# Gate vector's product before the first turn of x, half-turn copies and another order of the first K pieces, in a fused linear-attention and MLP kernel

## The chip, the cores and the metric

The kernel runs on one core of one Trainium2 chip. The metric is the device time of one execution in microseconds, as the median of several runs. Beside the timed runs there is one profiled execution, taken by the hardware profiler; its span is the time from the first to the last instruction, and its own device time is a little longer than the span. The engines are named as in the profile: PE (matmuls) and PEld (its weight loads), DVE (vector engine), ACT (scalar engine, activations), POOL, and SP, which here only issues DMAs.

## The reference

Two branches work on the same x (2048 rows of 640 features, bf16) and are mixed by a gate per row. Branch A is linear attention with 32 heads, branch B a spatial-shift mixer with an MLP. Shortened:

```python
x = A_x
g = sigmoid((x * gate_w).sum(-1, keepdims=True))

# A: linear attention
q, k, v = split(x @ wqkv)                       # 32 heads of 20
pq, pk = phi(q), phi(k)                         # phi(t) = where(t > 0, t + 1, exp(t)) + 1e-6
kv, z = pk^T v, sum(pk)                         # per head
a = ((pq @ kv) / (pq . z + 1e-6)) @ wo

# B: layernorm, w1, gelu, shifts along the sequence, w2, residual, layernorm, w3, gelu, w4
x1 = x + shifted(gelu(layernorm(x) @ w1)) @ w2
b = x1 + gelu(layernorm(x1) @ w3) @ w4

out = g * a + (1 - g) * b
```

The part that matters here is the very first: `k = x @ wk` and the gate's row sum `x . gate_w`, which the kernel computes as one extra column of the same product.

## The kernel before

The 2048 rows are 16 chunks of 128 (c = 0 to 15), the 640 features 5 groups of 128 (dc = 0 to 4). The order of the work is written out by hand: each engine does its instructions in program order, and waits are put in by the framework where tiles depend on each other.

**The start.** x chunk 0 and chunk 1 are loaded row by row into `x_sb` (line 123, SP's queue); the later chunks come already transposed by DMA into `xT` (line 126). The five row groups of the K weights `wk_sb` are loaded alternately from SP's and ACT's queue (line 129): rows 1 on SP, rows 0 and 2 on ACT, rows 3 on SP, rows 4 on ACT. The gate vector is loaded as `g5` (5 x 128) and put into the zeroed tile `g5z` by DVE (lines 205, 206).

**Fillers.** `warmup` (line 203) issues matmuls of constants into a PSUM pair that nobody reads. Five of 512 columns and one of 384 run while the first loads are under way; later one of 512 and one of 256 columns stand between the real matmuls.

**Turns.** K products need x with the features on the partitions. For chunks 0 and 1, PE turns x itself: `turn` (lines 210 to 221) multiplies each 128 x 128 block by the identity (line 214), features 0 and 1 into the first bank of a PSUM pair, features 2, 3 and 4 into the second. Two copies (line 219) bring them to `xT`: for chunk 0 both on DVE, for chunk 1 the first on DVE and the second on ACT. In chunk 0's turn, the product of `g5z` and the identity (line 217) puts the gate vector into the first bank behind features 0 and 1, and DVE copies it into column D of `wk_sb` (line 221).

**K pieces.** A piece (c, dc) is two matmuls (line 190) that add the product of feature group dc of chunk c to a PSUM pair; the second half has the gate column as its 321st. Each chunk needs five pieces. For chunks 0 and 1 the pieces are interleaved by a list, and chunk 1's turn stands in it ahead of the third piece. Then `k_evac` (line 193) copies the gate's column with ACT and applies phi: ACT's exp (line 182) and two DVE instructions (lines 183, 184). For chunks 2 to 15 all five pieces of a chunk run in a row. PSUM has four pairs in rotation; a pair is taken again when its readers are done.

After the 16 chunks follow the Q products (line 245), the products of phi(k) with x (line 345), and branch B, all as long rows of matmuls.

Of the kernel before, what the change touches and what calls it, by code (L numbers as in the profile page):

```python
# [16 lines left out]
def kernel(  # L17
# [13 lines left out]
    nc = tc.nc  # L31
    P = 128
    S, D = A_x.shape[1], A_x.shape[2]
# [6 lines left out]
    DC = D // P  # L40
# [29 lines left out]
    def pair():  # L70
        return ps.tile([P, 2, 512], F32, name="pp")
# [17 lines left out]
    ident = const.tile([P, P], BF16)  # L89
    g5 = const.tile([DC, P], BF16)  # L90
    g5z = const.tile([P, P], BF16)
# [20 lines left out]
    wk_sb = st1.tile([P, DC, D + 16], BF16)  # L112
    gT = wk_sb
    xT = st1.tile([P, DC, S], BF16)
# [71 lines left out]
    def k_mm(pt, c, dcs, first=0, last=DC - 1):  # L186
        for dc in dcs:
            for hf in range(2):
                n = HD + hf
                nc.tensor.matmul(pt[:, hf, 0:n], lhsT=xT[:, dc, c * P:(c + 1) * P],  # L190
                                 rhs=wk_sb[:, dc, hf * HD:hf * HD + n], start=(dc == first), stop=(dc == last))
# [5 lines left out]
    k0_order = (1, 0, 2, 3, 4)  # L197
    warm = pair()
    one = nc.const_aps.tensor(1.0, (P, TS), BF16)

    def warmup(n, w=TS, pt=warm):
        for i in range(n):
            nc.tensor.matmul(pt[:, 1, 0:w], lhsT=one[:, 0:P], rhs=one[:, 0:w], start=True, stop=True)
# [1 line left out]
    nc.vector.memset(g5z[:], 0.0)  # L205
    nc.vector.tensor_copy(g5z[0:DC, :], g5[:])
    warmup(5)
    warmup(1, 3 * P)

    def turn(pt, c, split, copies):  # L210
        parts = ((0, split), (split, DC))
        for h, (a, b) in enumerate(parts):
            for dc in range(a, b):
                nc.tensor.matmul(pt[:, h, (dc - a) * P:(dc - a + 1) * P], lhsT=x_sb[:, c, dc * P:(dc + 1) * P],
                                 rhs=ident[:], start=True, stop=True)
        if c == 0:
            nc.tensor.matmul(pt[:, 0, 2 * P:2 * P + DC], lhsT=g5z[:], rhs=ident[:, 0:DC], start=True, stop=True)
        for h, (a, b) in enumerate(parts):
            copies[h](xT[:, a:b, c * P:(c + 1) * P], pt[:, h, 0:(b - a) * P].rearrange("p (c s) -> p c s", c=b - a))  # L219
            if c == 0 and h == 0:  # L220
                copies[h](wk_sb[:, :, D], pt[:, 0, 2 * P:2 * P + DC])

    tp = pair()
    turn(tp, 0, 2, (nc.vector.tensor_copy, nc.vector.tensor_copy))
    warmup(1, TS)
    kps = [pair(), pair()]
    for n, (c, dc) in enumerate(((0, 1), (0, 0), (0, 2), (0, 3), (1, 1), (1, 0), (0, 4), (1, 2), (1, 3), (1, 4))):
        if n == 2:
            turn(warm, 1, 2, (nc.vector.tensor_copy, nc.scalar.copy))
        if n == 1:  # L230
            warmup(1, 2 * P, kps[1])
        k_mm(kps[c], c, (dc,), first=k0_order[0], last=k0_order[-1])
    for c in range(2):
        k_evac(kps[c], c)
    for c in range(2, NCH):
        pt = pair()
# [481 lines left out]
```

## Time and profile before

| what | value |
|---|---|
| median of 3 runs | 262.87 us |
| the runs | 261.99, 262.87, 265.05 us |
| profiled execution, its own time | 261.71 us |
| profiled execution, span | 260.0 us |
| granted PE clock over the span | 1.000 |
| PE idle before a DMA-fed turn of chunk 0 / chunk 1 (weight load, line 214) | 0.51 / 0.22 us |
| DMA engines, mean busy share in the first 10 us, moved | 2.11 MB at 211 GB/s |
| a K matmul of 320 columns (line 190), mean of 160 | 300 ns |

The duration of a matmul in the profile includes its way through the array; in a row of them the next starts before the one ahead has ended, so the distance between starts is shorter than the duration. In the timeline, equal instructions that follow each other are merged into one line with their count; the first two numbers are the start and the time to the end of the last of them, in microseconds from the start of the span. The bracket at a line's end gives the idle time of that engine before it and whose end released it.

### The profile page before, as it was taken

Reading aid. Unit: us, or ns where it says so; the run is one execution under the profiler, and the core shown is the slowest. Engines: PE = TensorE matmul, PEld = TensorE weight load, DVE = VectorE, ACT = ScalarE, POOL = GpSimd, SP = SyncE. Lnnn points to the kernel's source line nnn. Section 1 sums busy time; section 2 is a strip of 40 time slices with the busy share of each in tenths; the row PEclk is TensorE's granted clock in tenths of the full one; section 3 lists DMA queues with packets and bytes.
Section 4 is the critical chain, followed back from the end, with each engine's and each line's share of the span. In section 5 each row is a group of like instructions: output and inputs, shape, how many; then the busy total and the mean of one; then the engine's idle time right before and its main releaser. Section 6 shows DMA issues by size and latency. Waiting matters only on the chain.

```text
span 260.0 us, 4128 instructions
## 1 busy us (share of the span) xinstructions
PE 254.9 (98%) x1590; PEld 151.0 (58%) x1613; DVE 148.1 (57%) x274; ACT 107.7 (41%) x166; POOL 32.2 (12%) x87
## 2 busy tenths in 40 slices
PE   8999999999999999999999999999999999999995
PEld 4777555788754644565464566455565546465543
DVE  2688678899998888399300398600287610125132
ACT  2655554385787547431343323342322344342100
POOL 3000040023411140023000131000122000000000
PEclk9999999999999999999999999999999999999999
DMA  7999995026661877964122124214123412211011
GB/s 217 191 204 377 363 331 203 0 43 123 122 115 31 231 77 160 283 187 84 20 43 40 20 53 96 76 23 62 20 50 74 101 20 43 48 38 57 21 50 50
DMA packets 57557, 28.27 MB, mean 109 GB/s; under 512 B 45506, under 2 KB 56770, under 8 KB 57538
## 3 DMA queue, kind: packets, MB, share of 16 engines
q1 hardware_dynamic: 57096, 27.52, 43.2%
q10 hardware_dynamic: 442, 0.49, 0.5%
q8 instruction: 12, 0.20, 0.3%
q14 instruction: 7, 0.06, 0.1%
HBM read 13.03 MB, written 3.60 MB: 64 GB/s over the span
## 4 chain that ended last, share of the span: by engine, by line
PE 96%; DMA 1%; issue 1%; SPq 0%; DVE 0%
PE pp L541 21%; PE pp L580 16%; PE pp L491 8%; PE pp L345 8%; PE pp L522 8%; PE pp L245 8%; PE pp L400 8%; PE pp L190 8%; PE pp L616 5%; DMA wk_sb<-in_A_wqkv_dram 1%; PE pp L551 1%; PE pp L572 1%; PE pp L433 1%; PE pp L419 1%; SPq L123 0%
## 5 line engine op out<-in xcount | busy, mean ns | idle before, releaser
L541 PE MATMUL pp<-lnxT,w_sb 128*128 128x512 bf16 x249 | 59.8, 379 | 0.6
L543 ACT ACTIVATE h<-pp 128x1024 bf16<-128x1024 f32 (+1 forms) x28 | 26.9, 962 | 56.0 <-PE pp L541 56.0
L580 PE MATMUL pp<-h,w_sb 128*128 128x512 bf16 (+1 forms) x228 | 42.4, 343 | 0.3
L541 PEld LDWEIGHTS <-w_sb 128*128 128x128 bf16 x260 | 25.2, 98 | 26.9
L494 DVE TENSOR_TENSOR x<-pp,x_sb 128x640 f32<-128x640 f32 x16 | 13.0, 815 | 40.0 <-PE pp L491 40.0
L580 PEld LDWEIGHTS <-w_sb 128*128 128x128 bf16 x234 | 22.7, 98 | 19.5 <-issue 1.0
L182 ACT ACTIVATE e<-pp 128x640 bf16<-128x640 f32 (+1 forms) x26 | 21.5, 827 | 9.5 <-PE pp L245 9.5
L308 POOL TENSOR_SCALAR rstd<-mv 128x1 f32<-128x1 f32 (+2 forms) x22 | 9.2, 416 | 128.8 <-DVE mv L314 127.9
L522 PE MATMUL pp<-m_sb,pqT 128*128 128x320 bf16 x160 | 24.3, 299 | 0.0
L528 DVE SCALAR_TENSOR_TENSOR x<-pp,gate,x 128x640 f32<-128x640 f32 x16 | 14.1, 882 | 17.4 <-PE pp L522 11.9
L491 PE MATMUL pp<-w_sb,hsT 128*128 128x320 bf16 x160 | 23.9, 299 | 0.0
L190 PE MATMUL pp<-wk_sb,xT 128*128 128x320 bf16 (+1 forms) x160 | 22.4, 300 | 0.2
L345 PE MATMUL pp<-x_sb,pk 128*128 128x320 bf16 (+1 forms) x160 | 22.0, 300 | 0.0
L245 PE MATMUL pp<-xT,hsT 128*128 128x512 bf16 x98 | 21.6, 379 | 0.1
L345 PEld LDWEIGHTS <-pk 128*128 128x128 bf16 x160 | 18.8, 117 | 3.2
L491 PEld LDWEIGHTS <-hsT 128*128 128x128 bf16 x160 | 15.6, 98 | 8.2 <-issue 0.2
L522 PEld LDWEIGHTS <-pqT 128*128 128x128 bf16 x160 | 15.7, 98 | 7.7
L593 DVE SCALAR_TENSOR_TENSOR oc<-pqT,omg,x 128x640 bf16<-128x640 bf16 x12 | 10.5, 878 | 16.8 <-DMA pqT<-hx 16.8
L190 PEld LDWEIGHTS <-xT 128*128 128x128 bf16 x160 | 15.5, 98 | 6.8 <-DVE xT L219 0.6
L400 PE MATMUL pp<-lnxT,w_sb 128*128 128x512 bf16 x77 | 17.9, 379 | 0.2
L245 PEld LDWEIGHTS <-hsT 128*128 128x128 bf16 x100 | 11.8, 118 | 9.7
L309 POOL TENSOR_TENSOR rstd<-rstd,mhalf 128x1 f32<-128x1 f32 (+2 forms) x22 | 16.8, 765 | 1.8
(89 smaller groups left out, 250.7 us busy)
## 6 DMA issues: line engine op xcount, KB each, us to landing
x_sb<-in_A_x_dram SPq DMA_DIRECT2D x1, 2240.0 KB
out_dram<-oc SPq DMA_DIRECT2D x14, 160.0 KB, 1.8
w_sb<-in_B_w_dram SPq DMA_DIRECT2D x1, 2160.0 KB
w_sb<-in_B_w_dram SPq DMA_DIRECT2D x1, 2080.0 KB
wo_sb<-in_A_wo_dram SPq DMA_DIRECT2D x6, 160.0 KB
hsT<-in_A_wqkv_dram SPq DMA_DIRECT2D x1, 800.0 KB
m_sb<-in_A_wqkv_dram SPq DMA_DIRECT2D x1, 800.0 KB, 12.7
w_sb<-in_B_w_dram SPq DMA_DIRECT2D x1, 800.0 KB
```

The lines of the kernel that those rows point to most:

```text
L182: nc.scalar.activation(ev, src, ACT.Exp)
L190: nc.tensor.matmul(pt[:, hf, 0:n], lhsT=xT[:, dc, c * P:(c + 1) * P], rhs=wk_sb[:, dc, hf * HD:hf * HD + n], start=(dc == first), stop=(dc ...
L245: nc.tensor.matmul(pt[:, t % 2, :], lhsT=wq_sb[:, dc, :].rearrange("p (m j) -> p j m", j=DC)[:, j], rhs=xT[:, dc, t * TS:(t + 1) * TS], st ...
L309: nc.gpsimd.tensor_tensor(out_ap, out_ap, mhalf[:, 0:out_ap.shape[1]], op=ALU.pow)
L345: nc.tensor.matmul(pt[:, hf, 0:HD + hf], lhsT=w, rhs=x_sb[:, c, hf * HD:(hf + 1) * HD + hf], start=(c == 0), stop=(c == NCH - 1))
L400: nc.tensor.matmul(pt[:, i, :], lhsT=w, rhs=lnxT[t][:, dc, :], start=(dc == 0), stop=(dc == DC - 1))
L491: nc.tensor.matmul(pt[:, hf, 0:HD], lhsT=hsT[:, fc, 2 + c * P:2 + (c + 1) * P], rhs=w2_sb[:, fc, hf * HD:(hf + 1) * HD], start=(fc == 0), ...
L522: nc.tensor.matmul(pt[:, hf, 0:HD], lhsT=pqT[:, j, c * P:(c + 1) * P], rhs=m_sb[:, j, hf * HD:(hf + 1) * HD], start=(j == 0), stop=(j == D ...
L528: nc.vector.scalar_tensor_tensor(x1, pt[:, :, 0:HD], gate[:, c:c + 1], x1, op0=ALU.mult, op1=ALU.add)
L541: nc.tensor.matmul(pt[:, k, :], lhsT=w3_sb[:, dc, fc * P:(fc + 1) * P], rhs=lnT[:, dc, :], start=(dc == 0), stop=(dc == DC - 1))
L543: nc.scalar.activation(h2[:, 2 * i * TS:(2 * i + n) * TS], pt[:].rearrange("p h e -> p (h e)")[:, 0:n * TS], ACT.Gelu_apprx_tanh)
L580: nc.tensor.matmul(dst, lhsT=w4_sb[:, fc, d * P:(d + 1) * P], rhs=st[t]["h2"][:, fc * TS + a:fc * TS + b], start=False, stop=(fc == FF - 1))
```

## The change

Three things are changed in the stretch between the first fillers and the K pieces of chunk 1.

The gate vector's product no longer belongs to chunk 0's turn. It stands ahead of it, writes into the pair `warm` that the fillers use, and is followed by a filler of 128 columns in place of the one of 384. DVE's copy into column D of `wk_sb` is issued there too.

`turn` issues the copy of each half right behind that half's products instead of behind all five, and the first half takes feature 1 before feature 0 (`range(split - 1, -1, -1)`).

In the list of K pieces, (1,1) and (1,0) stand ahead of (0,3), and (1,2) ahead of (0,4). The 256-column filler stands behind the second piece instead of ahead of it.

```diff
     warmup(5)
-    warmup(1, 3 * P)
+    nc.tensor.matmul(warm[:, 0, 0:DC], lhsT=g5z[:], rhs=ident[:, 0:DC], start=True, stop=True)
+    warmup(1, P)
+    nc.vector.tensor_copy(wk_sb[:, :, D], warm[:, 0, 0:DC])
 
     def turn(pt, c, split, copies):
-        parts = ((0, split), (split, DC))
-        for h, (a, b) in enumerate(parts):
-            for dc in range(a, b):
+        for h, dcs in enumerate((range(split - 1, -1, -1), range(split, DC))):
+            a = min(dcs)
+            for dc in dcs:
                 nc.tensor.matmul(pt[:, h, (dc - a) * P:(dc - a + 1) * P], lhsT=x_sb[:, c, dc * P:(dc + 1) * P],
                                  rhs=ident[:], start=True, stop=True)
-        if c == 0:
-            nc.tensor.matmul(pt[:, 0, 2 * P:2 * P + DC], lhsT=g5z[:], rhs=ident[:, 0:DC], start=True, stop=True)
-        for h, (a, b) in enumerate(parts):
-            copies[h](xT[:, a:b, c * P:(c + 1) * P], pt[:, h, 0:(b - a) * P].rearrange("p (c s) -> p c s", c=b - a))
-            if c == 0 and h == 0:
-                copies[h](wk_sb[:, :, D], pt[:, 0, 2 * P:2 * P + DC])
+            n = len(dcs)
+            copies[h](xT[:, a:a + n, c * P:(c + 1) * P], pt[:, h, 0:n * P].rearrange("p (c s) -> p c s", c=n))
...
-    for n, (c, dc) in enumerate(((0, 1), (0, 0), (0, 2), (0, 3), (1, 1), (1, 0), (0, 4), (1, 2), (1, 3), (1, 4))):
+    for n, (c, dc) in enumerate(((0, 1), (0, 0), (0, 2), (1, 1), (1, 0), (0, 3), (1, 2), (0, 4), (1, 3), (1, 4))):
         if n == 2:
             turn(warm, 1, 2, (nc.vector.tensor_copy, nc.scalar.copy))
+        k_mm(kps[c], c, (dc,), first=k0_order[0], last=k0_order[-1])
         if n == 1:
             warmup(1, 2 * P, kps[1])
-        k_mm(kps[c], c, (dc,), first=k0_order[0], last=k0_order[-1])
```

## The prediction

> **What bounds the kernel now.** I read the page's busy shares and the chain of waits first, then the timeline of the first 8 us, because every instruction that the change touches runs there. The page:
>
> ```profile
> span 260.0 us, 4128 instructions
> PE 254.9 (98%) x1590; PEld 151.0 (58%) x1613; DVE 148.1 (57%) x274; ACT 107.7 (41%) x166; POOL 32.2 (12%) x87
> PE 96%; DMA 1%; issue 1%; SPq 0%; DVE 0%
> ```
>
> TensorE (PE) sets the end; only work that moves the start of its unbroken stream can matter. The chain in order of time says where that stream starts:
>
> ```profile
> 1.71 0.42 SPq L123
> 2.18 3.81 DMA wk_sb<-in_A_wqkv_dram
> 6.03 21.14 PE pp L190 x154
> ```
>
> From 6.03 on PE never stops for long, and the piece that starts there had waited for the load of wk_sb rows 3 (issued at 2.18, landed at 5.99). So what counts is one date: when PE has done the ten K pieces of chunks 0 and 1 and turns to chunk 2. Two matmuls make a piece; 21.14 us / 154 = 0.137 us each, so a piece is 0.275 us. Before, six matmuls lie ahead of 6.03 and 14 behind it: the date is 6.03 + 14 x 0.137 = 7.95 us. A shift of this date shifts everything behind it. The timeline ahead of it:
>
> ```profile
> 2.73 1.28 ACT L219 ACT_TABLE_LOAD   x1 [2.73 <-issue]
> ...
> 3.15 0.56 PEld L214 LDWEIGHTS <-x_sb 128*128 128x128 bf16 x5 [0.51 <-DMA x_sb<-in_A_x_dram]
> 3.24 0.74 PE L214 MATMUL pp<-ident,x_sb 128*128 128x128 bf16 x5
> ...
> 3.77 0.21 PE L217 MATMUL pp<-ident,g5z 128*128 128x5 bf16 x1
> ...
> 3.84 0.59 PE L203 MATMUL pp<-const-bfloat16-1.0 128*128 128x512 bf16 x1
> 4.04 0.42 DVE L219 CAST xT<-pp 128x256 bf16<-128x256 f32 x1 [1.63 <-PE pp L217]
> 4.39 0.17 DVE L221 CAST wk_sb<-pp 128x5 bf16<-128x5 f32 x1
> 4.46 0.55 DVE L219 CAST xT<-pp 128x384 bf16<-128x384 f32 x1
> 4.52 0.11 PEld L190 LDWEIGHTS <-xT 128*128 128x128 bf16 x2 [0.60 <-DVE xT L219]
> 4.53 0.45 PE L190 MATMUL pp<-wk_sb,xT 128*128 128x320 bf16 x2
> ...
> 5.24 0.28 PEld L214 LDWEIGHTS <-x_sb 128*128 128x128 bf16 x5 [0.22 <-DMA x_sb<-in_A_x_dram]
> 5.25 0.45 PE L214 MATMUL pp<-ident,x_sb 128*128 128x128 bf16 x5
> ...
> 5.74 0.42 DVE L219 CAST xT<-pp 128x256 bf16<-128x256 f32 x1 [0.73 <-PE pp L214]
> ...
> 6.19 0.48 ACT L219 CAST xT<-pp 128x384 bf16<-128x384 f32 x1 [2.18 <-DVE xT L219]
> ```
>
> Columns: start, duration, engine, line, operation, and in brackets the idle time before it and who ended it. Three things to see. The first copy of a turn starts only after the last product of the turn (4.04 after L217; 5.74 after the fifth product). Chunk 1's turn starts at 5.25 because its x has just landed. ACT's table load of 1.28 us waits for nothing and lies in dead time, 2.2 us before ACT's copy.
>
> **The change, part by part.** No DMA, no SP or POOL instruction moves and no work is added in sum; 256 columns of filler go, matmuls change place, and waits change.
>
> *Gate product first.* It goes behind the five fillers, where g5z has been ready since 2.42. The x rows land at 3.15 in any case and a 128-column filler fills until then, so the turn starts at 3.16 to 3.24 as now; I take 3.2. Its small DVE copy (0.17) lies beside the turn. Cost nothing: the wait for x hides it; without that cover it would be the 0.07 us between 3.77 and 3.84.
>
> *Features 1 and 0 copied apart, chunk 0.* Products there are 0.105 us apart ((3.77 - 3.24) / 5), the second ends about 3.51, and DVE follows 0.05 later (3.98 to 4.04): copy 3.56 to 3.98, half a microsecond sooner than now. But both halves of a turn lie in one PSUM pair, and in the changed program the third product waits for DVE's fourth instruction, which is this copy; now the five products run through. PE is held until 3.98 + 0.07 = 4.05 with the other three products, the 512-column filler and all K pieces queued behind it. Three products to 4.37, filler 0.22 (twice what the 256-column one keeps PE, 4.81 to 4.92), first piece at 4.6 against 4.53; second piece 4.87, the 256-column filler (0.11), and PE stands before chunk 1's turn at 5.25. That turn can't begin before 5.24 in either kernel. Part's sum: 0 to 0.05 us; the x landing swallows gain and loss alike.
>
> *The same, chunk 1.* Two products from 5.25 at 0.056 each; the second ends near 5.53, copy 5.57 to 5.99, third product 6.06. PE is held from 5.36, 0.69 us. Hidden by nothing: the 2.48 us of PE work behind it (five products 0.28, eight pieces 2.20) stands in the queue. What it removes: the wait for wk_sb rows 3 (5.81 to 6.03, 0.22 us), gone since those rows are needed later. Net +0.47.
>
> *Pieces (1,1) and (1,0) before (0,3).* Third to fifth product to 6.23, then (0,2), (1,1), (1,0), (0,3) to 7.32. The order costs nothing by itself; next is (1,2), which needs ACT's copy of features 2 to 4.
>
> *ACT's copy.* Today it has one wait, for DVE's copy, which implies PE's. After the change it has two: DVE's sixth instruction (copy of features 1 and 0) and PE's last product. The program puts the first of them ahead of the table load, so the load, which now runs at 2.73, starts only at 5.99 + 0.05. Queued behind it on ACT is the copy itself, and then the exps. Load 6.05 to 7.33, copy (0.48) 7.35 to 7.83, PE's (1,2) at 7.88 instead of 7.32: +0.56. Of the load's 1.28 us, 0.7 is covered by the four pieces; with fewer of them ahead it would be on the path whole. What the load takes when a wait precedes it this trace doesn't show at the start, so I bound it by its rows: nothing if it overlaps the wait after all, and 1.28 from this row:
>
> ```profile
> 67.46 1.28 ACT L380 ACT_TABLE_LOAD   x1
> 68.76 0.20 ACT L380 ACTIVATE nmr<-mhalf 128x1 f32<-128x1 f32 x1
> ```
>
> The next instruction starts 0.02 us after the load's end, so I take 1.28 with nothing behind it. [...]
>
> *Sum.* Four pieces remain, (1,2), (0,4), (1,3), (1,4): 7.88 + 4 x 0.275 = 8.98 against 7.95, **+1.03 us**. Behind it, chunk 0's chain ends later by the same: (0,4) done near 8.6, its exp and two DVE steps (0.71 + 0.33 + 0.82) end near 10.7, and the pair they free is wanted by chunk 4 at 8.98 + 2 x 1.37 = 11.7. So nothing is added, and no DMA wait of PE in the rest of the chain could take the delay back.
>
> On the profiled execution (span 260.0 and 1.71 around it, 261.71) this gives 262.7. The runs shown are 261.99, 262.87 and 265.05; the median of them and the profiled one is 262.43, so I forecast 262.43 + 1.03 = **263.5 us**, 0.4% over.
>
> **The clock.** The 512-column filler at 3.84 took 0.59 us, and the 256-column one at 4.81 took 0.27, with the next matmul 0.11 behind it: the slow start ends between 3.84 and 4.53. The change puts 0.64 us of idle PE (3.41 to 4.05) into just this stretch. The trace has no such gap there, so its cost is bounded by zero and by the slow start lasting as long again. [...] The slow start seen is 3.0 to 3.7 us (0.83 to 3.84 or 4.53); I take zero, since 2.6 us of unbroken fillers still stand ahead of the gap.
>
> **The rivals.**
> - *The full clock comes late* (slower). One more slow stretch as long as the first (0.83 to about 4.2, 3.4 us) lasts to about 7.65: pieces cost 0.53 until then. First piece 4.8, turn of chunk 1 at 6.08, its copy 6.53 to 6.95, load and ACT copy to 8.78, then four pieces from 8.84: 9.94, +2.0 us (0.8%). Two such stretches, to about 11.1: (1,2) at 9.5 and three slow pieces more, end 11.4, +3.45 us (1.3%). It decides from the point where a clock change falls behind 5.3, chunk 1's turn. For it: the gaps at 3.41, 5.36 and 7.32 fall into every such stretch. Against: PE is busy for four fifths of each. Chance 0.18, of which 0.08 for two stretches or more.
> - *The table load doesn't count* (it runs during the wait): only the held turn remains, 7.32 + 4 x 0.275 = 8.42, +0.47 us, 262.9. Against it: ACT takes its instructions in order here. Chance 0.12.
> - *The pair's wait doesn't bind* (the change does what its words say): PE goes through at 5.25, 2.48 us of work, rows 3 no longer waited for: 7.73, with ACT's load from 6.04 on still allowing (1,2) at 7.88 rather than 6.6, +1.0 again; with neither wait -0.2 us, 262.2. Chance of the latter 0.08. More than 0.22 can't be had: the landing of chunk 1's x at 5.24 stands.
>
> **How the numbers follow.** Forecast 0.62, rivals 0.18, 0.12, 0.08. About 1%, 2.6 us, is what a measurement of this kernel can tell from no change (the three runs lie 3 us apart). Faster by over 1% has no case, only scatter: 0.03. Slower by over 1% is the two-stretch case (0.08) and scatter on the +1 and +2 cases (0.09): 0.17. Within 1%: 0.80. The range runs from the -0.2 case (262.2) to the two-stretch case (265.9): 262.2 to 265.9, which leaves the tails of scatter out.
>
> **What would show it.** In the changed profile: the table load near 6.05, released by DVE; ACT's copy near 7.35; PE idle of about 0.6, 0.7 and 0.5 us ahead of the third product of each turn and of (1,2), and none at 6.03; chunk 1's turn still at 5.25; chunk 2's first K matmul near 9.0. Wrong it would be if the load still lies at 2.7, if the third product follows the second at once, or if matmuls after 4.6 lie 0.27 us apart.

## The result, and the profile after

The changed kernel took 263.66 us in the median of 22 runs (263.04 to 264.96), the kernel before 262.21 us in 22 runs beside it. The ratio is 1.0056, 95% interval 1.0041 to 1.0072: 0.56% slower, about 1.5 us, inside the 1% that was forecast as most likely. Seven of the 22 runs of the changed kernel lie above 264.3 us and one of those before; what lies behind the spread is taken up under the clock and stays in part open. The profiled execution took 263.43 us, with a span of 261.7 us against 260.0.

First the chain of waits of the changed kernel, in order of time, up to the Q products (start, duration, and what the end of the program waited for there):

```profile
3.54 0.02 issue
3.56 0.43 DVE xT L219
4.00 0.04 issue
4.04 0.48 PE pp L216 x3
4.52 0.43 PE pp L203
4.95 0.98 PE pp L190 x4
...
6.04 0.13 PE pp L216 x2
6.16 0.02 issue
6.18 0.43 DVE xT L219
6.62 0.02 issue
6.64 0.02 ACTq L219
6.66 0.03 issue
6.69 1.28 ACT L219
7.97 0.01 issue
7.99 0.49 ACT xT L219
8.47 0.05 issue
8.52 20.34 PE pp L190 x148
28.86 0.21 PE pp L243
```

The lines shown begin at 3.54. Before, this chain ran over the load of wk_sb rows 3 to 6.03 and was PE's alone from there. Now it leaves PE twice after 3.5 us. At 3.56 it goes through DVE's copy of chunk 0's features 1 and 0, and the three other products wait. At 6.18 it goes through the same copy of chunk 1, and from there not back to PE but into ACT: the table load at 6.69, ACT's copy at 7.99, and only then piece (1,2) at 8.52. The load and the copy are 1.8 us of a path on which neither stood before.

The timeline of the same execution shows who waited for whom (the bracket is the engine's idle time before it and who ended it):

```profile
4.04 0.48 PE L216 MATMUL pp<-ident,x_sb 128*128 128x128 bf16 x3 [0.52 <-DVE xT L219]
...
4.31 0.63 PE L203 MATMUL pp<-const-bfloat16-1.0 128*128 128x512 bf16 x1
...
4.74 1.19 PE L190 MATMUL pp<-wk_sb,xT 128*128 128x320 bf16 x4
...
5.87 0.28 PE L216 MATMUL pp<-ident,x_sb 128*128 128x128 bf16 x2
6.18 0.42 DVE L219 CAST xT<-pp 128x256 bf16<-128x256 f32 x1 [1.07 <-PE pp L216]
6.66 0.33 PE L216 MATMUL pp<-ident,x_sb 128*128 128x128 bf16 x3 [0.52 <-DVE xT L219]
6.69 1.28 ACT L219 ACT_TABLE_LOAD   x1 [6.69 <-DVE xT L219]
6.83 1.25 PE L190 MATMUL pp<-wk_sb,xT 128*128 128x320 bf16 x8
7.99 0.48 ACT L219 CAST xT<-pp 128x384 bf16<-128x384 f32 x1
8.52 4.47 PEld L190 LDWEIGHTS <-xT 128*128 128x128 bf16 x34 [0.77 <-ACT xT L219]
8.52 4.67 PE L190 MATMUL pp<-wk_sb,xT 128*128 128x320 bf16 x33 [0.44 <-ACT xT L219]
```

All three stalls are there. The bracket's 0.52 counts from the modelled end of the second product; by an estimate from the starts PE could have issued the third one about 0.7 us sooner (the second at 3.21 plus the 0.107 between slow products gives 3.32, against 4.04). The table load has moved from 2.73, where it waited for nothing, to 6.69, where DVE's copy releases it. The eight matmuls at 6.83 are the pieces (0,2), (1,1), (1,0) and (0,3); behind them PE has nothing until ACT is done.

Two dates split the loss of this pair of profiles. Chunk 1's turn starts at 5.87 against 5.25. From there to the first Q product it takes 28.86 - 5.87 = 22.99 us, against 27.17 - 5.25 = 21.92 before (6.03 + 21.14 = 27.17). So 0.62 us come before the turn and 1.07 us from its start on. The 0.62 belongs to these two executions: in a second pair of profiles, shown under the clock, the turn starts at 5.58 in the changed kernel and at 5.79 in the kernel before. Behind the first Q product both take 232.8 us to the end of the span. The experiments therefore use the second difference, from chunk 1's first product to the first Q product; a late first part can't disturb it, unless PE is still slow in the turn itself.

### The profile page after: what moved, and what is told of

It reads as the page before. It is cut to its first block, busy times and chain, and to the rows that moved or that the text cites. A ratio compares the mean times of both kernels' runs of the same rounds, so it can differ in the third digit from the quotient of the medians.

```text
span 261.7 us, 4129 instructions
## 1 busy us (share of the span) xinstructions
PE 255.3 (98%) x1590; PEld 151.3 (58%) x1613; DVE 148.2 (57%) x274; ACT 107.5 (41%) x166; POOL 32.2 (12%) x87
## 4 chain that ended last, share of the span: by engine, by line
PE 97%; ACT 1%; issue 1%; DVE 0%; ACTq 0%
PE pp L539 21%; PE pp L578 16%; PE pp L489 8%; PE pp L343 8%; PE pp L520 8%; PE pp L243 8%; PE pp L398 8%; PE pp L190 8%; PE pp L614 5%; PE pp L203 1%; PE pp L549 1%; PE pp L570 1%; PE pp L431 1%; PE pp L417 1%; ACT L219 0%
```

## The experiments

The theory: two waits cost the time, the third product's wait for DVE in a turn, and the wait ahead of the table load. The rivals: the order of the pieces, the gate vector's product, and the clock.

**The table load alone.** One copy of a single column at the start makes ACT load its table there (at 2.73 in the profile):

```diff
+    nc.scalar.copy(nmr1[:, NCH:NCH + 1], mhalf[:, 0:1])
     nc.vector.memset(g5z[:], 0.0)
```

> The changed kernel with one ACT copy of a single column at the start, so that the table load comes before it and no longer behind a wait. Theory (the load is on the path): load at about 2.7 us, ACT's copy of chunk 1's features 2 to 4 near 7.05, PE's piece (1,2) directly behind (0,3), no PE idle there; chunk 2's first K matmul near 9.03 instead of 9.62, time 0.6 us below the changed kernel, about 0.85 above the kernel before. Rival (the load was covered, PE would have waited for something else): chunk 2 stays at 9.6, time as the changed kernel.

Measured: median 263.01 us in 11 runs (a twelfth took 963.27 us and is left out), 1.0038 of the kernel before (1.0008 to 1.0068), 0.65 us below the changed kernel. The runs fall into two groups, seven from 262.4 to 263.5 us and four from 264.5 to 264.8, so the median is a poor measure of the load. The profile fell on an execution of 264.48 us in which PE stayed slow until about 9.9 us (matmuls of the pieces 0.27 us apart from 7.17 to 9.58, 0.135 from 10.03 on), so its dates said nothing of the load. The same kernel again:

> The changed kernel with the early table load once more, for a profile with another date of the clock's rise (9.8 us in the first). Theory: PE's piece (1,2) follows (0,3) without idle time, and from the third product of chunk 1's turn to the first K matmul of chunk 2 it takes 0.17 us for the products and 8 pieces of 0.275, 2.37 us, where the changed kernel took 2.95 and 2.95 (6.66 to 9.62, 6.37 to 9.32): the load's price is 0.58. Rival: 2.9 us again.

The chain of waits of this second profile (263.09 us):

```profile
6.49 0.44 DVE xT L220
6.92 0.04 issue
6.96 0.33 PE pp L217 x3
7.29 21.26 PE pp L190 x156
28.55 0.22 PE pp L244
```

ACT is gone from the chain; PE runs through from 6.96. From the third product of chunk 1's turn to the first Q product it takes 28.55 - 6.96 = 21.59 us, where the changed kernel took 28.86 - 6.66 = 22.20. The load's place costs 0.61 us; the rival, that it was covered, falls. The hold in the turn is still there: DVE's copy stands in the chain. Of the 1.07 us, 0.46 are left for it and the new order.

**The held product.** Two edits take it away, one by undoing it, one by removing its reason. First, the copies go back behind all five products, while the gate product and the order of pieces stay as changed:

```diff
+        for h, dcs in enumerate((range(split - 1, -1, -1), range(split, DC))):
-            n = len(dcs)
+            a, n = min(dcs), len(dcs)
             copies[h](xT[:, a:a + n, c * P:(c + 1) * P], pt[:, h, 0:n * P].rearrange("p (c s) -> p c s", c=n))
```

> The changed kernel with the copies of a turn put back behind all five products; gate product first and the new order of pieces stay. Theory: no hold of PE inside the turns, ACT's copy has one wait again and the load lies at 2.7, the full clock comes before 4.6; chunk 1's turn at 5.25, its DVE copy 5.74 to 6.16, and piece (1,1) waits for it until 6.22; chunk 2's first K matmul near 8.14, 0.2 us above the kernel before. Rival (the new order or the gate product costs most): chunk 2 at 9 or later.

Measured: 262.58 us, 1.0009 (0.9978 to 1.0040), level with the kernel before; the interval is too wide to tell the 0.2 us that were expected. The timeline of this run, and behind it the end of its chain of waits:

```profile
2.73 1.28 ACT L220 ACT_TABLE_LOAD   x1 [2.73 <-issue]
...
5.43 0.28 PEld L216 LDWEIGHTS <-x_sb 128*128 128x128 bf16 x5 [0.41 <-DMA x_sb<-in_A_x_dram]
...
6.40 3.58 PE L190 MATMUL pp<-wk_sb,xT 128*128 128x320 bf16 x25 [0.25 <-DVE xT L220]
```

```profile
6.40 21.16 PE pp L190 x154
27.56 2.59 PE pp L244 x12
```

The load is back at 2.73 and chunk 1's turn again waits for its x, which landed 0.2 us later than in the first profile of before. Piece (1,1) waits 0.25 us for the copy of chunk 1's features, as worked out for the new order. From the turn to the first Q product: 27.56 - 5.43 = 22.13, 0.21 above the kernel before, where 0.19 was expected.

Second, the two halves of a turn lie in different PSUM pairs, with the copies apart as in the changed kernel:

```diff
-            a = min(dcs)
+            a, pt = min(dcs), pts[h]
...
-    turn(tp, 0, 2, (nc.vector.tensor_copy, nc.vector.tensor_copy))
+    turn((tp, kps[1]), 0, 2, (nc.vector.tensor_copy, nc.vector.tensor_copy))
...
-            turn(warm, 1, 2, (nc.vector.tensor_copy, nc.scalar.copy))
+            turn((warm, tp), 1, 2, (nc.vector.tensor_copy, nc.scalar.copy))
```

> The changed kernel with the two halves of a turn in different PSUM pairs. In this program the third product of a turn has no wait for DVE, and ACT's table load waits only for the copy of chunk 0's features 1 and 0. Theory: third product directly behind the second in both turns, clock up before 4.6, load from 4.0 to 5.3 beside other work, (1,1) at 6.05 behind the copy of chunk 1's features; chunk 2's first K matmul near 7.97, time within 0.2 us of the kernel before, 1.4 below the changed kernel. Rival (the late clock has another cause than the held turn): chunk 1's turn at 5.8 or later again, chunk 2 near 8.6.

Measured: 262.38 us, 1.0010 (0.9983 to 1.0036). Its chain of waits:

```profile
1.71 3.61 DMA x_sb<-in_A_x_dram
5.32 0.05 issue
5.36 0.30 PE pp L216 x2
5.66 0.02 issue
5.68 0.44 DVE xT L219
6.12 0.05 issue
6.17 21.16 PE pp L190 x154
27.32 2.81 PE pp L243 x13
```

No product waits inside a turn, and the only stop left is the copy ahead of (1,1). 27.32 - 5.36 = 21.96 us, the kernel before to within 0.04. ACT's load left the path as well: in this run's timeline it lies from 4.01 to 5.29, released by the copy of chunk 0, and ACT's copy starts only at 5.85. So the wait came with the two halves' common pair, not with copying them apart. What copying apart was able to bring shows here too. In chunk 0's turn it is nothing: chunk 1's turn waits for x until 5.3. In chunk 1's turn it is 0.17 us against the run with the copies behind (21.96 against 22.13), about what the new order costs.

**The order and the gate product, each alone in the kernel before.**

```diff
-    for n, (c, dc) in enumerate(((0, 1), (0, 0), (0, 2), (0, 3), (1, 1), (1, 0), (0, 4), (1, 2), (1, 3), (1, 4))):
+    for n, (c, dc) in enumerate(((0, 1), (0, 0), (0, 2), (1, 1), (1, 0), (0, 3), (1, 2), (0, 4), (1, 3), (1, 4))):
```

> The kernel before with the new order of K pieces alone. Theory: piece (1,1) stands where (0,3) stood and waits for DVE's copy of chunk 1's features (ends 6.16) until 6.22 instead of for wk_sb rows 3 until 6.03; nothing else changes; chunk 2's first K matmul 0.19 later, near 8.14, time 0.2 us above the kernel before. Rival (the order matters more, by ACT's copy or the evacuation of chunk 0): over 0.5 us.

Measured: 262.58 us, 1.0001 (0.9980 to 1.0023). From the turn to the first Q product 28.03 - 5.79 = 22.24; some of the turn's products were slow here (the five took 0.57 us, 0.45 in the kernel before), so the 0.2 us can't be told from this run alone. The interval reaches 0.6 us; it is the dates, 0.32 us above the kernel before with slow products in it, that speak against the rival of over half a microsecond.

```diff
-    warmup(1, 3 * P)
+    nc.tensor.matmul(warm[:, 0, 0:DC], lhsT=g5z[:], rhs=ident[:, 0:DC], start=True, stop=True)
+    warmup(1, P)
+    nc.vector.tensor_copy(wk_sb[:, :, D], warm[:, 0, 0:DC])
...
-        if c == 0:
-            nc.tensor.matmul(pt[:, 0, 2 * P:2 * P + DC], lhsT=g5z[:], rhs=ident[:, 0:DC], start=True, stop=True)
...
-            if c == 0 and h == 0:
-                copies[h](wk_sb[:, :, D], pt[:, 0, 2 * P:2 * P + DC])
```

> The kernel before with the gate vector's product moved ahead of chunk 0's turn alone. Theory: the turn's copies start 0.1 us sooner, the wait for chunk 1's x at about 5.25 takes it away again; chunk 2's first K matmul as in the kernel before for the same rise of the clock, time within 0.2 us of it. Rival (the gate product is what costs): 0.4 us or more.

Measured: 262.17 us, 1.0003 (0.9989 to 1.0017). The turn's first copy starts at 3.86 instead of 4.04, chunk 1's x lands and its turn starts at 5.50, and 27.36 - 5.50 = 21.86 us, 0.06 below the kernel before. The gate product costs nothing that can be told, and brings nothing.

**The clock.** Each kernel unchanged, profiled once more:

> The kernel before once more, for a second profile. [...] Rival: rise at 4.2 and chunk 2 at 7.95 as in the first profile.

> The changed kernel once more, for a second profile. [...] Rival (the gap fixes the rise): the rise at 5.5 to 5.7 and chunk 2 at 9.6 again.

What is called the clock here is read from the distance between the starts of equal matmuls in a row: for those of 320 columns 0.27 us while PE is slow (from 4.74 in the first profile of the changed kernel two take 0.74 us and three 1.01), 0.137 behind the rise (20.34 us for 148 from 8.52).

The kernel before took 262.48 us this time (span 260.8), the changed one 263.11 (span 261.4). The timeline of before, second profile:

```profile
4.53 0.71 PE L190 MATMUL pp<-wk_sb,xT 128*128 128x320 bf16 x2
...
5.04 0.42 PE L203 MATMUL pp<-const-bfloat16-1.0 128*128 128x256 bf16 x1
5.25 0.74 PE L190 MATMUL pp<-wk_sb,xT 128*128 128x320 bf16 x2
...
5.79 0.74 PE L214 MATMUL pp<-ident,x_sb 128*128 128x128 bf16 x5
```

The two matmuls of the first piece, 0.45 us in the first profile, take 0.71 here, and the turn's five products 0.74 instead of 0.45: PE was slow until at least 6.3 us though no product is held, and chunk 1's turn began at 5.79, 0.54 later. From there to the first Q product it took 27.93 - 5.79 = 22.14 us, 0.22 more than in the first profile, because the turn's own products were slow. The chain of the changed kernel's second profile:

```profile
6.40 1.28 ACT L219
...
8.22 20.34 PE pp L190 x148
28.56 0.21 PE pp L243
```

Here the rise lay near 5 (from the first piece at 4.81 to the next filler it took 0.66 us, where the same four matmuls took 1.07 with PE slow throughout, 4.68 to 5.75 in the early table load), the turn at 5.58 instead of 5.87, and 28.56 - 5.58 = 22.98 us. So the date of the rise differs from execution to execution in both kernels; the rival that the gap fixes it at 5.5 falls. The part after the turn, 22.99 and 22.98, is the same in both executions of the changed kernel, whose turns of chunk 1 began after the rise.

Three kernels fill the gaps. In the first, a 512-column filler is added between the second and third product of chunk 0's turn; in the second, the filler that stood behind the turn is moved there; in the third, chunk 1's turn gets two as well (the diff is the first one's, without the line that makes the pairs `kps` before the turn):

```diff
+            if c == 0 and h == 0:
+                warmup(1, TS, kps[1])
             n = len(dcs)
```

> The changed kernel with one 512-column filler between the second and third product of chunk 0's turn; all waits stay. Theory (the idle PE inside the slow start puts the full clock off): with the gap mostly filled, the clock rises before 4.7, chunk 1's turn starts at 5.25, the table load near 6.05, chunk 2's first K matmul near 9.0, time 0.6 us below the changed kernel. Rival (the clock comes when it comes, the gap has nothing to do with it): first K pieces at 0.27 us from matmul to matmul again, chunk 1's turn at 5.87, chunk 2 near 9.6, time as the changed kernel.

> The changed kernel with the 512-column filler that stood behind chunk 0's turn moved into the gap between its second and third product, so the count of instructions stays. All waits stay. Theory: chunk 1's turn at 5.25 to 5.4 in most runs, since the slow start's stretch has 0.2 us of idle PE in place of 0.6; chunk 2's first K matmul near 9.0, span near 261.1, median 0.3 to 0.6 us below the changed kernel, fewer runs above 264.3. Rival (the gap has nothing to do with the clock): median as the changed kernel.

> The changed kernel with fillers in the gaps ahead of both turns' third products: 512 columns in chunk 0's, 1024 in chunk 1's; all waits and the late load stay. Theory (idle PE in both gaps makes the clock miss its first stretch in a third of the runs): the runs lie together with none over 1 us above the lowest; from chunk 1's first product to the first Q matmul still 23.0 us as in the changed kernel (22.99 and 22.98), 1.07 above the kernel before. Rival (the late clock has nothing to do with the gaps): about a third of the runs again over 1 us above the lowest.

Measured, in this order: 263.80 us (1.0073, 1.0048 to 1.0098), 263.28 us (1.0044, 1.0014 to 1.0074), 263.57 us (1.0049, 1.0036 to 1.0062). In all three profiles the clock had risen by 4.6 (four matmuls of pieces, from 4.60, 4.22 and 4.43, took 0.54 us to the next filler) and the turn started at 5.32 to 5.42. That fits the theory but doesn't show it, since in kernels without these fillers the rise lay anywhere from about 3.7 (the gate product alone, where the 512-column filler at 3.62 took 0.42 us against 0.63 with PE slow throughout) to 9.9 us. From the turn to the first Q product it took 28.32 - 5.32, 28.41 - 5.41 and 28.41 - 5.42, 23.0 us each time, so the hold and the load stay whole. The times don't follow. The first is no faster than the changed kernel, though its profiled span is 0.6 us shorter (261.1; 3.0 us lay outside it, against 1.7 in the changed kernel's, which stays unexplained; its other five runs have spans of 261.8 us or more). The second's median is 0.4 us lower, but the intervals of the two ratios overlap, and three of its 12 runs lie above 264.3 again. Of the third's six runs none does, but the highest is 1.1 us above the lowest, just past what was expected, and six are few. Counted over the runs on record, but for one of 963 and one of 1547 us, those more than 1 us above the lowest run of their kernel in the same batch are 12 of 33 in the changed kernel and the early table load, 5 of 24 in the three with fillers, and 25 of 165 in kernels in which no product is held. They are more frequent with the gaps and not confined to them. Whether the gaps put the clock off in some runs is left open.

**An attempt at a better kernel.** Two pairs for a turn, and piece (0,4) ahead of (1,1), so that PE has work while chunk 1's first copy runs:

```diff
...
-    for n, (c, dc) in enumerate(((0, 1), (0, 0), (0, 2), (1, 1), (1, 0), (0, 3), (1, 2), (0, 4), (1, 3), (1, 4))):
+    for n, (c, dc) in enumerate(((0, 1), (0, 0), (0, 2), (0, 4), (1, 1), (1, 0), (0, 3), (1, 2), (1, 3), (1, 4))):
...
-        k_mm(kps[c], c, (dc,), first=k0_order[0], last=k0_order[-1])
+        k_mm(kps[c], c, (dc,), first=k0_order[0], last=(3, 4)[c])
```

> The kernel with two PSUM pairs for a turn, and piece (0,4) ahead of (1,1), so that PE has work while chunk 1's first copy runs. Theory (rows 4 of wk_sb have landed by then): the 0.24 us of idle PE ahead of (1,1) go; from chunk 1's first product to the first K matmul of chunk 2 it takes 0.28 + 8 x 0.275 = 2.48 us, where two pairs alone took 2.73 (5.36 to 8.09); time 0.2 us below two pairs alone, level with the kernel before or up to 0.2 below it. Rival (rows 4 land later than rows 3): PE waits ahead of (0,4) instead, 2.7 us again.

Measured: 262.29 us, 1.0000 (0.9990 to 1.0009). The expectation was wrong and its rival right:

```profile
2.24 4.14 DMA wk_sb<-in_A_wqkv_dram
6.38 0.04 issue
6.43 21.14 PE pp L190 x154
```

Rows 4 landed at 6.38, and PE stood ahead of (0,4) instead: 27.57 - 5.41 = 22.16 us, 0.2 more than with two pairs alone. No kernel tried here is faster than the one before.

## Why the prediction was right, point by point

*The sum.* Forecast were 263.5 us and +1.03; measured are 263.66 and +1.45. The time agrees better than its parts, and that is luck: the base was taken 0.22 us too high (262.43 against 262.21) and the change 0.42 too low. The profiled execution, forecast at 262.7, took 263.43.

*What bounds the kernel.* Right. Everything behind the first Q product took 232.8 us in both profiles, so the whole loss lies in the first 9 us, as forecast.

*The held third product in chunk 1's turn* (+0.47 net) and *ACT's copy behind the table load* (+0.56): right together, 1.07 and 1.06 in the two profiles of the changed kernel, against the first one of before, where 1.03 was forecast. The load by itself measured 0.61, which leaves 0.46 for the hold (forecast 0.47). The load lasted 1.28 us and ACT's copy began 0.02 us after it (7.97 to 7.99). Nothing more stood between the load and the copy, as behind the load at 67.46 in the kernel before, so the row was the right price.

*The new order*, costing nothing by itself behind the held turn: right, and with the hold undone it costs the 0.2 us that (1,1) waits for its copy (22.13 against 21.92). *The gate product*: right, nothing.

*Chunk 0's turn*, "0 to 0.05 us; the x landing swallows gain and loss alike": mis-sized where PE is still slow. The hold is where it was forecast (third product at 4.04, forecast 4.05), but the cover was worked out with pieces at full clock from 4.6 on. When PE is still slow, two pieces take 1.07 us, PE comes to chunk 1's turn after its x has landed, and nothing swallows the delay: with PE slow throughout, the turn came at 5.96 and 6.08 (changed turn, early table load) against 5.79 in the kernel before, 0.2 to 0.3 us. That may be part of the 0.4 us by which the medians differ beyond 1.07 (263.66 - 262.21 = 1.45); no run separates it from the spread of the clock.

*The clock*, "the slow start ends between 3.84 and 4.53" and "I take zero": the first holds for one execution, not for the kernel, as the second profile of before shows. So the trace showed one date of a value that moves, and zero was taken for its cost. One sign by which the prediction called itself wrong came true: in the first profile after, the matmuls of the first pieces still start 0.27 us apart behind 4.6, chunk 1's turn starts at 5.87 instead of 5.25, and chunk 2 at 9.62 instead of 9.0. For the rival of a late clock I gave 0.10 to one stretch more, +2.0 us. That a second slow stretch lasts as long as the first, 3.4 us, was an estimate from the one slow start seen; no run shows such a length, only dates of the rise from about 3.6 to 9.9. An execution of that kind was seen with the early table load (264.48 us). If the 7 of 22 runs above 264.3 are such, the chance was too small; no profile shows one of them, and what sets it isn't settled.

*The rivals* that the load doesn't count or that the pair's wait doesn't bind fell with the brackets of the profile after.

## What to carry to other kernels

Copying a tile in parts gained nothing here while the parts shared a buffer that the dependency tracking took as one: the third product waited for the copy of the first two (0.52 us of idle PE), and with the parts in two pairs no product waited. Look in the built program at what a copy waits for, and give the parts buffers of their own. And where an engine's first use brings a load with it, as ACT's did (1.28 us), issue a harmless first use early: here a second wait on the real first use went ahead of the load and brought it onto the path, with 0.61 of its 1.28 us.

## What the runs showed of the hardware

The date at which PE comes to full clock differs between executions of one program. By the spacing of the matmuls it lies between 3.84 and 4.53 us in the first profile of the kernel before and behind 6.3 in the second, at about 5.7 and 5.0 in the two of the changed one. The kernel with the early table load was profiled with the rise at about 6.3 and at 9.9, and its spans were 261.4 and 262.8 us. In the other profiles estimates from the spacing put it between about 3.6 (both gaps filled: a 512-column filler at 3.33 took 0.52 us, 0.63 with PE slow throughout) and about 6.0 (the order alone: the turn's five products at 5.79 took 0.57 us, 0.74 with PE slow throughout).

Whether idle time of PE puts the rise off no run here settles. The changed kernel and the one with the early table load hold the same products, the third of each turn (0.51 to 0.52 us of idle PE ahead of it), and in their four profiles the rise lies at about 5.7, 5.0, 9.9 and 6.3 us.

Chunk 1's x landed between 5.2 and 5.5 us in the profiles in which PE stood waiting for it (turns at 5.25 in the kernel before, at 5.50 with the gate product alone). Savings ahead of that landing can't show in any of them.
